# A fused retention and feed-forward kernel: four tiles of the first product by seven products of quarters in two more blocks, and early token sums on GpSimd

## The chip, the cores and the metric

The kernel runs on one core of a Trainium2 chip. The metric is the device time of one execution in microseconds (us); lower is better. A core has five engines that work side by side, each through its own instructions in order: TensorE (PE, matrix products; its weight loads are shown as PEld), VectorE (DVE), ScalarE (ACT), GpSimd (POOL), and SyncE (SP), which here only starts DMA transfers. Matrix products go to PSUM, which has eight banks. A bank can be written anew only when its last reader is done. GpSimd has no part in PSUM here; it works on SBUF alone. Engines wait for each other by semaphores.

## The reference

Two stages. First a retention recurrence over 4 batches, 8 heads, 768 steps and a head width of 64; then a feed-forward layer with a leaky activation over the 3072 tokens:

```python
state = gamma[None, :, None, None] * state + einsum('bhd,bhe->bhde', k[:, :, t], v[:, :, t])
y[:, :, t] = scale * einsum('bhd,bhde->bhe', q[:, :, t], state)
...
x = y.transpose(0, 2, 1, 3).reshape(3072, 512)
h = x @ w_in                                   # 512 -> 2048
g = maximum(h, 0.0) + alpha * minimum(h, 0.0)
out = g @ w_out                                # 2048 -> 512
```

Inputs and output are float32; the kernel computes its products in fp16 and sums them in float32.

## The kernel before

**Tiling.** The retention works in 12 units of 256 steps (three per batch), the feed-forward layer in 6 blocks of 512 tokens, so that a block has two units. While block n goes through its feed-forward products, the two units of block n+1 go through the retention between them. The main loop (line 1188) runs over n from 1 to 5 and writes out by hand in which order every engine gets its instructions.

**First product** (`ffn1`, line 616). Sixteen tiles of 128 features, each four matmuls of 128x512 into one PSUM bank. Behind each tile comes the activation: ACT writes relu(-h) into `hm` (line 648), DVE forms the activated tile in fp16 in `gt` (line 650). The tiles go in the order 0, 8, 1, 9, ... 7, 15, through a list of banks.

**Second product** (`ffn2_seven`, line 826). For blocks 1 to 5 the product of a 512-token block with `w_out` is cut into quarters (two halves of the tokens, features and columns) and done by seven products of quarters in place of eight, after Strassen and Winograd. Each is 16 matmuls of 128x256 (line 857), into the banks named `ox` and `oy`. It needs sums of quarters of the activated tokens, the token sums `gs` (`g_sums`, line 602), numbered 0 to 3; sum 1 needs sum 0, and sum 3 needs sum 1. The third product reads sum 1, the fourth sum 0, the fifth sum 2, the seventh sum 3. In `ffn1` sums 0 and 1 are made by DVE in two halves: over feature tiles 0 to 3 and 8 to 11 behind tile 11, and over the rest behind tile 15. Sum 2 follows in the middle of the second product and sum 3 late in it. Behind the second product ACT copies `ox` to `os` (line 877), which empties the bank for the fourth.

**First product of the last block** (`ffn1_mixed`, line 694). Eight of the 16 tiles are made one by one; the other eight, in two groups of four, by seven products of quarters each, every one of four 128x256 matmuls (line 761). A plan gives the order of tiles and steps: a number is a tile, `a[i]` is step i of a group. Steps 1 and 2 fill one bank, which is then activated as a pair of half tiles; step 1 is also copied by ACT into a second bank, in which steps 6, 7 and 4 add up; ACT copies it out behind 6 and behind 7; step 5 fills a third bank, to which step 3 adds. Two sums with the copies give the other two quarters. The steps need sums of weights (`in_sums`, line 574) and of tokens (`x_sums`, line 590), made by DVE. In the last block the one group's fourth quarter is summed on DVE into SBUF and activated by GpSimd (`prelu_pool`, line 666), and the activated tiles' intermediate results lie in buffers that loads no longer need.

**Retention in the loop.** At the start of an iteration GpSimd rescales k and q of the next two units (line 185, the first one behind `gate`, the block's last token sum) and casts v (`cast_v`, line 201); SP transposes them by DMA (line 205), starts loads, and moves parts of q (line 220). Behind the first of the seven products come the state sums of both units (line 284) and the scores (line 345); from there DVE (`tm`, line 301; `ss`, line 312), GpSimd (`tf`, line 313; copies `tg`, `th`) and ACT (its copies of the same) hand the running state from one to another. The units' results `y` (lines 384 and 398) are copied by ACT into `xT` (line 556), the input of the next block's first product. The next block's first product is begun (`begin`, line 1180) behind the second unit's result, by four matmuls that stand ahead of the sixth of the seven products.

Of the kernel before, what the change touches and what calls it, by code (L numbers as in the profile page):

```python
# [9 lines left out]
FP = mybir.dt.float32  # L10
F16 = mybir.dt.float16
# [11 lines left out]
def kernel(  # L23
# [25 lines left out]
    U = 256  # L49
# [524 lines left out]
    def in_sums(f, i, eng):  # L574

        if f not in win_sums:
            t = sbp.tile([128, H, 2 * D], FP, tag="ks", bufs=3, name=f"wi{f}")
            t = t.rearrange("p h x -> p (h x)").bitcast(F16)
            win_sums[f] = t.rearrange("p (i k c) -> p i k c", i=4, k=2)
        w = w_in_all.rearrange("p (k h) (j f) -> p k h j f", k=2, j=2)[  # L580
            :, :, :, :, 128 * f : 128 * f + 256
        ]
        a11, a21, a12, a22 = (w[:, k, :, j, :] for k in range(2) for j in range(2))
        s1, s2, s3, s4 = (win_sums[f][:, x] for x in range(4))
        o, a, b, op = (
            (s1, a21, a22, ADD), (s2, s1, a11, SUB), (s3, a11, a21, SUB), (s4, a12, s2, SUB)
        )[i]
        return eng.tensor_tensor(out=o, in0=a, in1=b, op=op)

    def x_sums(n, eng):  # L590

        xs = sbp.tile([128, H, 2 * D], FP, tag="ks", bufs=3, name=f"xs{n}")
        xs = xs.rearrange("p h x -> p (h x)").bitcast(F16)
        xs = xs.rearrange("p (i k t) -> p i k t", i=4, k=2)
        x_sum[n] = xs
# [6 lines left out]
    def g_sums(n, i, lo, hi):  # L602
# [10 lines left out]
        last_g.append(nc.vector.tensor_tensor(out=o, in0=a, in1=b, op=op))  # L613
        return last_g[-1]

    def ffn1(n, banks, apart=0):


        turns = [(f, 2, ul, ul + 1) for ul in range(2) for f in range(0, apart, 2)]
        rest = range(apart, NFT)  # L620
        if apart == 0:
            rest = [f + x for f in range(HF) for x in (0, HF)]
        turns += [(f, 1, 0, 2) for f in rest]
        gt = None
        for i, (f0, nf, lo, hi) in enumerate(turns):
            hps = ps(banks[i % len(banks)], "hps").rearrange("p (f t) -> p f t", f=nf)
            parts = [(f, lo, hi) for f in range(nf)]
            if n > 1 and i == 0:
                parts = [(0, 0, 1), (0, 1, 2)]
            for f, ul, uh in parts:  # L630
                for hp in range(4):
                    nc.tensor.matmul(  # L632
                        out=hps[:, f, U * (ul - lo) : U * (uh - lo)].rearrange(
                            "p (u t) -> p u t", t=U
                        ),
                        lhsT=w_in_all[:, hp, 128 * (f0 + f) : 128 * (f0 + f) + 128],
                        rhs=xT[n][:, ul:uh, hp, :],
                        start=(hp == 0),
                        stop=(hp == 3),
                    )  # L640
# [7 lines left out]
            nc.scalar.activation(out=hm, in_=hps, func=RELU, bias=0.0, scale=-1.0)  # L648
# [29 lines left out]
    def prelu(n, f0, lo, hi, hps):  # L678

        nf = hps.shape[1]  # L680
        hm = hms[turn[0] % 4].rearrange("p m e -> p (m e)").rearrange("p (f t) -> p f t", f=nf)
        turn[0] += 1
        nc.scalar.activation(out=hm, in_=hps, func=RELU, bias=0.0, scale=-1.0)
        for f in range(nf):
            nc.vector.scalar_tensor_tensor(
                out=gts[n][:, f0 + f, U * lo : U * hi],
                in0=hm[:, f, :],
                scalar=oma_sb[:, f0 + f : f0 + f + 1],
                in1=hps[:, f, :],
                op0=MULT,  # L690
                op1=ADD,
            )

    def ffn1_mixed(n, plan, banks):
# [12 lines left out]
            return room.pop()  # L707

        def copied(i):
            t = space()  # L710
            nc.scalar.activation(out=t, in_=i, func=COPY, bias=0.0, scale=1.0)
            return t

        hms.extend(space() for _ in range(4))
        for item in plan:
            if isinstance(item, int):
                hps = ps(banks.pop(0), "hps").rearrange("p (f t) -> p f t", f=1)
                for hp in range(4):
# [28 lines left out]
            def x(k, ul):  # L747
# [6 lines left out]
                4: lambda: (bg, w(1, 1), xs[:, 3], False),  # L754
                5: lambda: (bv, wi[:, 0], xs[:, 0], True),
                6: lambda: (bg, wi[:, 1], xs[:, 1], False),
                7: lambda: (bg, wi[:, 2], xs[:, 2], False),
            }[i]()
            for m in range(2):
                for k in range(2):  # L760
# [16 lines left out]
            elif i in (5, 7):  # L777
# [410 lines left out]
    for n in range(1, NBLK):  # L1188
        more = n + 1 < NBLK
        u0 = 2 * (n + 1)  # L1190
        if n > 1:
            gen = begun
            if more:
                for u in (u0, u0 + 1):
# [2 lines left out]
                        behind(i, gate)  # L1197
                    rescale(G, u, 1, 0, 8)
                    turn_dma(u)
                    cast_v(G, u)  # L1200
                    if u > u0:
                        load(u + 1, "qv")
                    else:
                        load(u + 2, "k")
                    move_q(u)
                    tick(gen, 8)
            tick(gen)
            if not more:
                for i in (2, 4):
# [5 lines left out]
        if more and u0 >= MID:  # L1215
# [38 lines left out]
            halves_out(u1, (4, 5), evict=False)  # L1254
            begun = begin(n + 1)
            take_y(u1, (0, 1))
            state_copy(s11, part=1)
            if n == NBLK - 2:
                in_sums(6, 0, V)
                in_sums(6, 1, V)  # L1260
                x_sums(n + 1, V)
                in_sums(4, 0, V)
                in_sums(4, 1, V)
        elif more:
            tick(gen, 16)
            sum_mm(u0, (2, 3))
# [36 lines left out]
        if n == NBLK - 2:  # L1303
            in_sums(6, 2, V)
            in_sums(6, 3, V)
            in_sums(4, 2, V)
            in_sums(4, 3, V)


# [28 lines left out]
```

## Time and profile before

| what | us |
|---|---|
| median of 3 runs | 198.91 |
| lowest and highest of the runs | 198.54 and 199.42 |
| the profiled execution | 198.86 |
| its span, first to last instruction | 196.9 |
| ACT, relu of the first product, 80 of them, mean | 0.597 |
| DVE, token sum over all 8 pairs of tiles (128x2048, fp16) | 1.22 |

The profile is of one execution. Its page gives the busy time of each engine, the chain of work that ended last, and groups of like instructions; from the trace one can ask for a stretch of time, engine by engine. In a group's row stand the source line, the engine, the operation, output and inputs with their shapes, and how often; behind the bar the busy time, the mean duration in nanoseconds, and the idle time of the engine ahead of it with what ended it. In a row of the timeline stand the start and the duration, both in us, and in brackets an idle time ahead of it. In the chain in order of time stand the start, the duration and the work. The granted TensorE clock was 0.997 over the span.

### The profile page before, as it was taken

The page shows a single profiled execution, that of the slowest core. Times are in us where ns is not written, and L with a number is a line of the kernel's source. Part 1 is how long each engine was busy: PE and PEld are TensorE (multiplying, and loading weights), DVE is VectorE, ACT ScalarE, POOL GpSimd, SP SyncE. Part 2 cuts the span into 40 slices and gives each one's busy share as a digit, 9 for nine tenths or more (in the row PEclk, how much of TensorE's full clock was granted, in tenths as well). Part 3 has the DMA queues.
Part 4 walks back from the last instruction along what each step waited for, and adds up shares of the span by engine and source line. Part 5 has one row for each costly group of instructions (what it writes and reads, how often), then busy time and mean ns, then how long its engine had stood idle before and what let it go on. Part 6 is the DMA issues. An engine that isn't in the chain of part 4 may idle for free.

```text
span 196.9 us, 6085 instructions
## 1 busy us (share of the span) xinstructions
PE 189.3 (96%) x2529; PEld 128.8 (65%) x2529; DVE 156.3 (79%) x259; ACT 115.4 (59%) x199; POOL 106.1 (54%) x113
## 2 busy tenths in 40 slices
PE   6688999999999999999999999999999999999993
PEld 2356645568467688744688744788644788865882
DVE  7698987517698998289988389977489996999983
ACT  4458665349187668467467476467466486678110
POOL 3176897499549544970077980076970180039300
PEclk9999999999999999999999999999999999999998
DMA  5999999998879989898988899929865010400014
GB/s 156 313 317 380 374 381 377 293 180 136 211 192 200 286 197 265 213 311 175 213 203 209 256 201 191 222 65 225 256 122 126 17 57 3 160 3 0 0 65 152
DMA packets 90026, 37.92 MB, mean 193 GB/s; under 512 B 57984, under 2 KB 87696, under 8 KB 90000
## 3 DMA queue, kind: packets, MB, share of 16 engines
q1 hardware_dynamic: 88768, 36.45, 69.2%
q0 software_dynamic: 1056, 1.05, 3.6%
q8 instruction: 20, 0.33, 0.6%
q10 hardware_dynamic: 176, 0.04, 0.1%
q14 instruction: 6, 0.05, 0.1%
HBM read 27.31 MB, written 6.29 MB: 171 GB/s over the span
## 4 chain that ended last, share of the span: by engine, by line
PE 90%; SPq 4%; DMA 3%; DVE 0%; issue 0%; POOL 0%; DVEq 0%
PE hps L632 36%; PE ox L857 16%; PE oy L857 12%; PE ops L809 7%; SPq L165 4%; PE hps L719 4%; PE sp L761 3%; DMA vs<-in_v_dram 3%; PE y L533 1%; PE y L384 1%; PE trb L230 1%; PE st L284 1%; PE sca L466 1%; PE ov L857 1%; PE ow L857 1%; PE oz L857 1%
## 5 line engine op out<-in xcount | busy, mean ns | idle before, releaser
L632 PE MATMUL hps<-xT,win 128*128 128x512 f16 (+1 forms) x396 | 71.5, 338 | 0.3 <-DVE ss L423 0.3
L650 DVE SCALAR_TENSOR_TENSOR gt<-hm,oma,hps 128x512 f16<-128x512 f32 (+1 forms) x96 | 59.4, 656 | 12.1 <-issue 4.3
L648 ACT ACTIVATE hm<-hps 128x512 f32<-128x512 f32 x80 | 47.6, 597 | 24.6 <-PE hps L632 22.5
L632 PEld LDWEIGHTS <-win 128*128 128x128 f16 x396 | 38.1, 98 | 31.0 <-POOL win L978 0.4
L857 PEld LDWEIGHTS <-gs 128*128 128x128 f16 x320 | 31.0, 98 | 3.7
L857 PEld LDWEIGHTS <-gt 128*128 128x128 f16 x240 | 22.9, 98 | 4.0
L333 POOL CAST tg<-tm 64x256 f16<-64x256 f32 x12 | 4.8, 396 | 34.3 <-DVE tm L301 22.3
L185 POOL TENSOR_TENSOR kdq<-qs,tab 128x1024 f16<-128x1024 f32 (+1 forms) x12 | 20.2, 1686 | 3.0 <-DVE wsum L572 2.3
L185 POOL TENSOR_TENSOR kdq<-ks,tab 128x1024 f16<-128x1024 f32 (+1 forms) x12 | 20.2, 1686 | 2.6 <-PE y L515 2.6
L857 PE MATMUL ox<-wout,gt 128*128 128x256 f16 x144 | 17.3, 273 | 0.0
L857 PE MATMUL oy<-wsum,gs 128*128 128x256 f16 x144 | 17.2, 273 | 0.0
L556 ACT ACTIVATE xT<-y 128x512 f16<-128x512 f32 x22 | 14.9, 744 | 3.1 <-PE y L533 2.0
L201 POOL CAST vx<-vs 128x1024 f16<-128x1024 f32 (+1 forms) x13 | 12.6, 970 | 6.7 <-DMA vs<-in_v_dram 6.7
L809 PE MATMUL ops<-wout,gt 128*128 128x512 f16 x64 | 15.3, 380 | 0.0
L613 DVE TENSOR_TENSOR gs<-gt 128x1024 f16<-128x1024 f16 (+1 forms) x14 | 13.0, 934 | 0.2
L877 ACT ACTIVATE cu<-oy 128x512 f32<-128x512 f32 x10 | 6.0, 597 | 10.6 <-PE oy L857 10.1
L236 ACT ACTIVATE kq<-trb 128x1024 f16<-128x1024 f16 x8 | 8.2, 1023 | 6.3 <-PE trb L230 6.3
L313 POOL TENSOR_TENSOR tf<-ss,tab 128x256 f32<-128x256 f32 x10 | 10.3, 1028 | 2.5 <-DVE ss L312 1.3
L881 DVE TENSOR_TENSOR os<-ox,cu 128x512 f32<-128x512 f32 x5 | 3.4, 687 | 10.1 <-PE ox L857 10.1
L670 POOL TENSOR_SCALAR hn<-qc,oma 128x256 f32<-128x256 f32 x4 | 4.5, 1138 | 12.4 <-DVE qc L785 12.3
L809 PEld LDWEIGHTS <-gt 128*128 128x128 f16 x64 | 5.8, 98 | 6.0
L424 POOL TENSOR_TENSOR tf<-ss,tab 128x256 f32<-128x256 f32 x6 | 5.9, 980 | 7.1 <-DVE ss L423 7.1
(119 smaller groups left out, 293.1 us busy)
## 6 DMA issues: line engine op xcount, KB each, us to landing
qs<-in_q_dram SPq DMA_DIRECT2D x9, 512.0 KB, 5.4
ks<-in_k_dram SPq DMA_DIRECT2D x32, 128.0 KB, 3.5
vs<-in_v_dram SPq DMA_DIRECT2D x32, 128.0 KB, 4.6
early<-in_moe_w_in_dram SPq DMA_DIRECT2D x7, 512.0 KB, 7.5
out_dram<-os SPq DMA_DIRECT2D x9, 256.0 KB, 2.5
early<-in_moe_w_out_dram SPq DMA_DIRECT2D x4, 512.0 KB, 7.0
out_dram<-ot SPq DMA_DIRECT2D x4, 512.0 KB, 3.8
ks<-in_k_dram SPq DMA_DIRECT2D x6, 256.0 KB, 6.1
```

The costliest lines, as they stand in the source:

```text
L165: nc.sync.dma_start(out=t[nm[0]][:, h, :], in_=src[b, h, U * c : U * c + U, :].rearrange("h (p r) d -> p h (r d)", r=2),)
L185: return eng.tensor_tensor(out=kdq[:, t, :, h0:h1, :].rearrange("p r h d -> p h r d"), in0=staged[u]["kq"[t]][:, h0:h1, :].rearrange("p h ...
L201: eng.tensor_copy(out=o, in_=i)
L236: nc.scalar.activation(out=kq.rearrange("p (x a) i -> p x a i", x=4)[:, :, 2 * hh : 2 * hh + 2, :], in_=trb.rearrange("p (x a i) -> p x a ...
L313: nc.gpsimd.tensor_tensor(out=t, in0=ss, in1=dec, op=MULT)
L556: nc.scalar.activation(out=o, in_=i, func=COPY, bias=0.0, scale=1.0,)
L613: last_g.append(nc.vector.tensor_tensor(out=o, in0=a, in1=b, op=op))
L632: nc.tensor.matmul(out=hps[:, f, U * (ul - lo) : U * (uh - lo)].rearrange("p (u t) -> p u t", t=U), lhsT=w_in_all[:, hp, 128 * (f0 + f) : ...
L648: nc.scalar.activation(out=hm, in_=hps, func=RELU, bias=0.0, scale=-1.0)
L650: nc.vector.scalar_tensor_tensor(out=gt[:, f0 + f, U * lo : U * hi], in0=hm[:, f, :], scalar=oma_sb[:, f0 + f : f0 + f + 1], in1=hps[:, f, :],
L809: nc.tensor.matmul(out=opss[tq], lhsT=gt[:, ft, 128 * tq : 128 * tq + 128], rhs=w_out_all[:, ft, :], start=(ft == 0), stop=(ft == NFT - 1),)
L857: nc.tensor.matmul(out=o[1][m], lhsT=lhs(f, m), rhs=rhs(f), start=(first and f == 0 and (m == 0 or o[0] is None)), stop=(f == HF - 1), ski ...
```

## The change

In blocks 3 and 4 the first product becomes `ffn1_mixed`: twelve tiles one by one, and tiles 4, 5, 12 and 13 by seven products of quarters. The group's way is "d": the fourth quarter is summed by DVE into the bank that steps 1 and 2 have left, and activated as the other quarters are. The sums of weights for this group are made once, by DVE during block 2's first product, into a buffer of their own, and block 5 uses them too; there its own four sums go. The token differences for blocks 3 and 4 are four DVE instructions in buffers of the score masks (`x_sums_apart`), and their last one is now what the rescales wait for. The early half of token sums 0, 1 and 2 is made by GpSimd (`first_sums`), in blocks 2, 3 and 4: behind tile 11. In blocks 3 and 4 that is ahead of tiles 6, 14, 7 and 15; the other half of sums 0 and 1 stays on DVE behind the last tile. The cast of v of the next block's first unit goes from GpSimd to ACT and stands earlier. Step 1 stands ahead of the sixth of the seven products, and tile 0 ahead of the seventh. The banks of the twelve tiles, in the plan's order, are 2, 3, 7, 5, 0, 2, 3, 7, 5, 6, 7, 1; those of the group are 6, 4 and 1.

```diff
@@ in_sums @@
         if f not in win_sums:
-            t = sbp.tile([128, H, 2 * D], FP, tag="ks", bufs=3, name=f"wi{f}")
-            t = t.rearrange("p h x -> p (h x)").bitcast(F16)
-            win_sums[f] = t.rearrange("p (i k c) -> p i k c", i=4, k=2)
+            if f == 4:
+                win_sums[f] = sbp.tile([128, 4, 2, U], F16, tag="wi4", name="wi4")
+            else:
...
+    def x_sums_apart(n):
+
+        b = xT[n].rearrange("p j (k a) t -> p j k a t", k=2)
+        t = [
+            sbp.tile([128, 512], F16, tag=f"m2{i % 2}{i // 2}", bufs=2, name=f"xs{i}")
+            for i in range(4)
+        ]
+        xs = x_sum[n] = [x.rearrange("p (k t) -> p k t", k=2) for x in t]
+        for o, x, y in (
+            (xs[0], b[:, 1, 0], b[:, 0, 0]),
+            (xs[1], b[:, 1, 1], xs[0]),
+            (xs[2], b[:, 1, 1], b[:, 1, 0]),
+            (xs[3], b[:, 0, 1], xs[1]),
+        ):
+            i = nc.vector.tensor_tensor(out=o, in0=x, in1=y, op=SUB)
+        return i
+
+    def first_sums(n):
+
+        for i in range(3):
+            g_sums(n, i, 0, 4, nc.gpsimd)
@@ ffn1 @@
-                lo = 0 if apart or f0 < NFT - 1 else 4
-                hi = HF if f0 == NFT - 1 else 4
-                g_sums(n, 0, lo, hi)
-                g_sums(n, 1, lo, hi)
+                if apart:
+                    g_sums(n, 0, 0, HF)
+                    g_sums(n, 1, 0, HF)
+                elif f0 < NFT - 1:
+                    first_sums(n)
+                else:
+                    g_sums(n, 0, 4, HF)
+                    g_sums(n, 1, 4, HF)
@@ ffn1_mixed @@
         for item in plan:
+            if item == "first":
+                first_sums(n)
+                continue
...
-                if (f, 5) in sums and (f, 7) in sums:
+                if (f, 5) in sums and (f, 7) in sums and "d" in item[3]:
+                    h22 = ps(at[0], "h22").rearrange("p (f t) -> p f t", f=2)
+                    nc.vector.tensor_tensor(
+                        out=h22, in0=sums.pop((f, 5)), in1=sums.pop((f, 7)), op=ADD
+                    )
+                    done.append((f + HF, 1, 2, h22))
...
         for t in done:
             prelu(n, *t)
+        if n < NBLK - 1:
+            g_sums(n, 0, 4, HF)
+            g_sums(n, 1, 4, HF)
@@ the plan and begin @@
+    a = steps(4, 6, 4, 1, "d")
+    PLAN = [a[1], 0, a[2], 8, a[6], 1, a[5], 9, a[7], 2, 10, a[3], 3, a[4], 11, "first", 6, 14, 7, 15]
+    BANKS = (2, 3, 7, 5, 0, 2, 3, 7, 5, 6, 7, 1)
+    MIXED = (3, 4)
...
+        if n in MIXED:
+            gen = ffn1_mixed(n, PLAN, BANKS)
+            tick(gen, 3)
+            return gen
@@ the main loop @@
-                    cast_v(G, u)
+                    if u > u0 or n not in MIXED:
+                        cast_v(G, u)
...
+            if n == 2:
+                tick(gen, 4)
+                for i in range(4):
+                    last_g.append(in_sums(4, i, V))
...
-            g_sums(n, 2, 0, HF)
+            g_sums(n, 2, 4, HF)
...
             take_y(u1, (0, 1))
+            if n + 1 in MIXED:
+                tick(begun, 1)
...
-                in_sums(4, 0, V)
-                in_sums(4, 1, V)
+            if n + 1 in MIXED:
+                cast_v(A, u0 + 2)
+                gate = x_sums_apart(n + 1)
+                tick(gen, 16)
+                tick(begun, 4)
```

More of the change, by code (lines that the diff above doesn't have):

```diff
@@ L576, in in_sums @@
         if f not in win_sums:
-            t = sbp.tile([128, H, 2 * D], FP, tag="ks", bufs=3, name=f"wi{f}")
-            t = t.rearrange("p h x -> p (h x)").bitcast(F16)
-            win_sums[f] = t.rearrange("p (i k c) -> p i k c", i=4, k=2)
+            if f == 4:
+                win_sums[f] = sbp.tile([128, 4, 2, U], F16, tag="wi4", name="wi4")
+            else:
+                t = sbp.tile([128, H, 2 * D], FP, tag="ks", bufs=3, name=f"wi{f}")
+                t = t.rearrange("p h x -> p (h x)").bitcast(F16)
+                win_sums[f] = t.rearrange("p (i k c) -> p i k c", i=4, k=2)
         w = w_in_all.rearrange("p (k h) (j f) -> p k h j f", k=2, j=2)[
@@ L594, in x_sums @@
         xs = xs.rearrange("p (i k t) -> p i k t", i=4, k=2)
-        x_sum[n] = xs
+        x_sum[n] = [xs[:, i] for i in range(4)]
         b = xT[n].rearrange("p j (k a) t -> p j k a t", k=2)
@@ L600, in x_sums, with g_sums @@
         eng.tensor_tensor(out=xs[:, 3], in0=b[:, 0, 1], in1=xs[:, 1], op=SUB)
-    def g_sums(n, i, lo, hi):
+    def x_sums_apart(n):
[13 more added lines that the diff above has]
+        return i
+    def g_sums(n, i, lo, hi, eng=None):
         if n not in gsums:
@@ L612, in g_sums @@
         )[i]
-        last_g.append(nc.vector.tensor_tensor(out=o, in0=a, in1=b, op=op))
+        last_g.append((eng or nc.vector).tensor_tensor(out=o, in0=a, in1=b, op=op))
         return last_g[-1]
+    def first_sums(n):
+        for i in range(3):
+            g_sums(n, i, 0, 4, nc.gpsimd)
     def ffn1(n, banks, apart=0):
@@ L680, in prelu @@
         nf = hps.shape[1]
-        hm = hms[turn[0] % 4].rearrange("p m e -> p (m e)").rearrange("p (f t) -> p f t", f=nf)
-        turn[0] += 1
+        if n == NBLK - 1:
+            hm = hms[turn[0] % 4].rearrange("p m e -> p (m e)")
+            turn[0] += 1
+        else:
+            hm = sbp.tile([128, TB], FP, tag="hm", bufs=3, name="hm")
+        hm = hm.rearrange("p (f t) -> p f t", f=nf)
         nc.scalar.activation(out=hm, in_=hps, func=RELU, bias=0.0, scale=-1.0)
@@ L709, in copied @@
         def copied(i):
-            t = space()
+            if n == NBLK - 1:
+                t = space()
+            else:
+                t = sbp.tile([128, 2, HM], FP, tag="cu", bufs=OUTS["cu"], name="cu")
             nc.scalar.activation(out=t, in_=i, func=COPY, bias=0.0, scale=1.0)
             return t
-        hms.extend(space() for _ in range(4))
+        if n == NBLK - 1:
+            hms.extend(space() for _ in range(4))
         for item in plan:
+            if item == "first":
+                first_sums(n)
+                continue
             if isinstance(item, int):
@@ L753, in ffn1_mixed @@
                 3: lambda: (bv, wi[:, 3], x(1, 1), False),
[L754 to L757, printed above, removed]
+                4: lambda: (bg, w(1, 1), xs[3], False),
+                5: lambda: (bv, wi[:, 0], xs[0], True),
+                6: lambda: (bg, wi[:, 1], xs[1], False),
+                7: lambda: (bg, wi[:, 2], xs[2], False),
             }[i]()
@@ L782, in ffn1_mixed @@
                     sums[f, 5] = copied(bv) if p else bv
-                if (f, 5) in sums and (f, 7) in sums:
+                if (f, 5) in sums and (f, 7) in sums and "d" in item[3]:
[4 more added lines that the diff above has]
+                    done.append((f + HF, 1, 2, h22))
+                elif (f, 5) in sums and (f, 7) in sums:
                     h22 = space()
```

2 lines of the change are left out of this document (removed).

## The prediction

> **What bounds the kernel now.** I read the page's busy shares and its chain of work first, then the chain in order of time around block 3, then the queues of VectorE (DVE), GpSimd (POOL) and ScalarE (ACT) there.
>
> ```profile
> PE 189.3 (96%) x2529; PEld 128.8 (65%) x2529; DVE 156.3 (79%) x259; ACT 115.4 (59%) x199; POOL 106.1 (54%) x113
> PE 90%; SPq 4%; DMA 3%; DVE 0%; issue 0%; POOL 0%; DVEq 0%
> ```
> ```profile
> 107.06 0.54 PE hps L632 x4
> 107.60 1.75 PE oy L857 x16
> 109.34 1.75 PE ox L857 x16
> 111.09 13.39 PE hps L632 x64
> 124.48 1.78 PE ox L857 x16
> ...
> 127.16 1.85 PE ox L857 x16
> 129.02 1.75 PE oy L857 x16
> 130.76 0.87 PE ox L857 x8
> ...
> 135.32 0.27 PE y L384 x17
> ```
>
> TensorE is the chain: from block 2 on its matmuls follow each other without a gap worth naming. So work taken from it counts only if nothing else then comes late, and the other queues must be tested for slack. In these rows 107.60 is the sixth product of block 2, 109.34 its seventh, 111.09 the first product of block 3, 124.48 the first of block 3's seven products, and 130.76 the first half of its fourth.
>
> ```profile
> 125.93 0.69 DVE L613 TENSOR_TENSOR gs<-gt 128x1024 f16<-128x1024 f16 x1
> 126.65 0.69 DVE L613 TENSOR_TENSOR gs<-gs,gt 128x1024 f16<-128x1024 f16 x1
> 127.26 0.41 DVE L301 TENSOR_TENSOR tm<-tf,st 128x256 f32<-128x256 f32 x1
> ...
> 128.92 0.42 DVE L301 TENSOR_TENSOR tm<-tf,st 128x256 f32<-128x256 f32 x1 [0.19 <-POOL tf L313]
> ```
> ```profile
> 127.74 0.39 POOL L333 CAST tg<-tm 64x256 f16<-64x256 f32 x1 [10.47 <-DVE tm L301]
> 128.28 0.61 POOL L313 TENSOR_TENSOR tf<-ss,tab 128x256 f32<-128x256 f32 x1
> ```
> ```profile
> 129.38 0.41 ACT L329 ACTIVATE tg<-tm 64x256 f16<-64x256 f32 x1
> 129.82 0.60 ACT L877 ACTIVATE os<-ox 128x512 f32<-128x512 f32 x1
> ```
>
> This is the tight place. Behind the first product the queues hand one thing round: the two token sums of the second half (DVE, 125.93 and 126.65), tm (DVE, 127.26), tf (POOL, 128.28), tm again (DVE, 128.92), its copy tg (ACT, 129.38), and only then, in ACT's queue, the copy os that empties the bank of ox. It ends at 129.82 + 0.60 = 130.42, and the fourth product needs that bank at 130.76: slack 0.34. POOL was idle for 10.47 us before that chain; the change fills that idle time.
>
> **The change part by part.** *TensorE, removed.* In each of blocks 3 and 4, four tiles of four 128x512 matmuls become seven products of four 128x256 matmuls: 16 go, 28 come. From the rows, 256 columns cost 1.75/16 = 0.109 and 512 cost (13.39 - 4 x 0.109)/60 = 0.216. So 16 x 0.216 - 28 x 0.109 = 0.39 us less per block, 0.8 for two. That is all there is to win: 198.86 - 0.8 = 198.1.
>
> *DVE, added in the first product.* Durations come from block 5, where the same steps run already:
>
> ```profile
> 177.92 0.69 DVE L790 TENSOR_TENSOR sp<-sp,qc 128x512 f32<-128x512 f32 x1
> 178.53 0.86 DVE L685 SCALAR_TENSOR_TENSOR gt<-qc,oma,sp 128x256 f16<-128x256 f32 x2
> 179.31 0.74 DVE L685 SCALAR_TENSOR_TENSOR gt<-qc,oma,hps 128x512 f16<-128x512 f32 x1
> 179.97 0.86 DVE L685 SCALAR_TENSOR_TENSOR gt<-qc,oma,sp 128x256 f16<-128x256 f32 x2
> ```
>
> Start to start: a sum in PSUM 0.61, a pair of halves 0.78, a whole tile 0.66. Four tiles at 0.66 give way to four pairs at 0.78 and two sums at 0.61, +1.7; the two early token sums (0.69 each) leave, -1.4. The total hardly moves, but the order does. The steps a2, a6, a5 give DVE little while TensorE runs them, and the adds and pairs come together behind a7. Step by step: TensorE ends the sixth product at 109.34, tile 0 (0.86) at 110.2, the seventh product at 111.96; a2, 8, a6, 1, a5, 9 (three of 0.44, three of 0.86) end at 115.86; a7, 2, 10, a3, 3, a4, 11, 6, 14 (three of 0.44, six of 0.86) end at 122.34.
>
> ```profile
> L648 ACT ACTIVATE hm<-hps 128x512 f32<-128x512 f32 x80 | 47.6, 597 | 24.6 <-PE hps L632 22.5
> L236 ACT ACTIVATE kq<-trb 128x1024 f16<-128x1024 f16 x8 | 8.2, 1023 | 6.3 <-PE trb L230 6.3
> 107.13 1.34 ACT L556 ACTIVATE xT<-y 128x512 f16<-128x512 f32 x2
> ```
>
> DVE gets tile 9 one relu (0.60) later, at 116.5, and has no gap from there: 9, sum, 2, pair, 10, sum, 3, pair, pair, 11 = 4 x 0.66 + 2 x 0.61 + 3 x 0.78 + 0.74 = 6.94, with some 0.2 for hand-overs, so tile 11 is done at 123.65. **Tile 7 takes tile 11's bank (7)**, and TensorE is there at 122.34: it waits 1.5, to about 123.85 with the hand-over. Tiles 7 and 15 end at 125.6, where before it was 124.48.
>
> *POOL, added: three token sums over half the tiles.* They start behind tile 11, at 123.7.
>
> ```profile
> L572 POOL TENSOR_TENSOR wsum<-wout 128x2048 f16<-128x2048 f16 x1 | 4.1, 4064 | 0.0
> 107.83 1.90 POOL L185 TENSOR_TENSOR kdq<-ks,tab 128x1024 f16<-128x1024 f32 x1
> 130.65 1.22 DVE L613 TENSOR_TENSOR gs<-gt 128x2048 f16<-128x2048 f16 x1
> 130.91 1.44 POOL L313 TENSOR_TENSOR tf<-ss,tab 128x256 f32<-128x256 f32 x1 [0.17 <-POOL tg L333]
> ```
>
> The nearest row, fp16 pairs, gives 4.06/2 = 2.03 each; the other sum of 1024 took 1.90. I take 2.03 and keep 1.90 and, from tf's 0.61 for 256, 2.45 as ends. The last two rows show more: tf, 0.61 alone, took 1.44 when it met an fp16 sum on DVE and ended 0.47 behind that sum, so the two kinds of sum exclude each other. Here the POOL sums run 123.7 to 125.75 and to 127.8. DVE's sum over the second half, due at 127.0 behind tile 15, waits to 127.8 and runs to 128.5; the third POOL sum follows to 130.5; DVE's other one starts there. Before, it started at 126.65 and os ended 3.77 later; now os ends at 134.27, and the fourth product, with the old hand-over of 0.2, starts at 134.4 in place of 130.76: **+3.65 per block**. The bank wait and a wait of the third product lie inside that. Behind it nothing of DVE or POOL is nearer than before, so it is not won back. Blocks 3 and 4 have the same rows: 7.3.
>
> The Trainium skill speaks against this edit (SBUF — State Buffer, section "SBUF: two separate sides"): a DVE instruction with two SBUF inputs and a GpSimd one hold their shared ports for the whole instruction, and the other blocks. By it the sum is the one above; without it the POOL sums would end at 129.8, DVE's would lie beside them, and tg, tf, tm, tg and os would follow to 132.4: 1.8 per block. The Trainium skill (GPSIMD Engine Reference, section "3.1 Elementwise — side-by-side cycle accounting") has 4497 ns for an fp32 sum of 2048; by half of that, 2.25, the estimate would be some 1.3 us higher.
>
> *Block 2.* Its early sums go to POOL and four sums of weights come to DVE, three tiles earlier.
>
> ```profile
> L588 DVE TENSOR_TENSOR wi<-win 128x512 f16<-128x512 f16 x4 | 1.7, 416 | 0.0
> ```
>
> Four of 0.42 against two of 0.69 is +0.3, in front of the reuse of a bank; 0.2 taken, 0 and 0.6 kept. POOL's three sums fit there: it is done with its casts well before the eighth tile. In block 5 those weight sums leave DVE:
>
> ```profile
> 168.84:181.42 12.58, 12.58 (x86) 8.21 (x85) 12.51 (x28) 10.06 (x19) 5.92 (x6) 1.00 0.16 58
> ```
>
> The columns are the stretch, then TensorE, weight loads and DVE busy: TensorE is gapless at 12.58 of 12.58, so this wins nothing.
>
> *Moved.* The cast of v goes to ACT (about 1.02 by the 1024 row) between the copies of xT, over at 108.47, and tile 0's relu: with a copy of 0.60, a small one and the old copy of 0.60, ACT is free near 111.0, and DVE reaches tile 0 by 111.6, ahead of the seventh product's end. Nothing waits. The rescales on POOL stay behind the gate, now the last token difference, four DVE instructions of 0.42 behind xT: 110.2 in place of 107.83, so they end near 118.8, still 5 us ahead of the sums.
>
> ```profile
> 112.33 2.30 SPq L205 DMA_TRANSPOSE kq<-kdq x1
> ...
> 124.18 1.29 SPq L220 DMA_DIRECT2D qf<-kq x2
> ```
>
> Their consumers in SP's queue (transposes, then loads, then the moves of q) slide by about 2 us, the last q to 127.5 plus its landing; it is read at 135.32 or later. Hidden; if not, each us over costs one.
>
> Sum: 198.86 + 7.3 + 0.2 = 206.4, rounded down to **206.2** for the shorter POOL row. The profiled execution took 198.86, its span 196.9, and the median of the runs is 198.91, so nothing is to be shifted.
>
> **The rivals.** (a) *Only the bank wait.* The POOL sums and DVE's do not exclude each other, or POOL is faster on contiguous fp16. Then per block the bank's 1.5 less 0.39 stays, up to 1.8 with the late tf: 198.86 + 2.2 to 3.6 + 0.2 = 201.3 to 202.7. For it: no row shows two such sums of 1024 meeting. Against it: the 1.44. (b) *Nothing waits*, the other side: the late order of DVE is caught up, as in block 5, where DVE is busy 12.51 of 12.58 and TensorE has no gap. It decides at bank 7: DVE must end tile 11 by about 122.2, 1.4 us sooner than I count, and the POOL sums must be done by 127.7. Then 198.1, the whole saving. Against it: 6.94 us of instructions stand between, and the wait for tile 7's activation is already met today, the 1.78 at 124.48 where other products take 1.75. (c) *POOL slower* (2.45 each): 1.3 more per block, 208.9.
>
> **How the numbers follow.** The forecast has 0.52, (a) with what lies between it and the forecast 0.25, (b) 0.16, (c) 0.03; 0.04 is left for a gain from a source that I do not see. A difference under 0.5%, about 1.0 us, can't be told from none here, so (b) counts as the same. Faster 0.04, same 0.16, slower 0.80. The range takes in (a) and the bounds of the POOL sum short of (c): 200.8 to 208.2.
>
> **What would show it.** Right: tile 7's first matmul waits over 1 us for tile 11's activation; each POOL token sum takes about 2.0; a DVE token sum behind them waits or is stretched; the fourth product starts late behind os. Wrong: first product of 12.9 us without gap, or POOL sums near 1 us, or tm within 2 us of the last tile's activation.

## The result and the profile after

The changed kernel takes **207.83 us** (median, 207.42 to 208.05) against 199.16 (198.54 to 199.45) for the kernel before in the same comparison: a ratio of **1.044, interval 1.040 to 1.047**. It is slower, where the forecast was 206.2 with a range of 200.8 to 208.2. The profiled execution took 208.05, its span is 206.0, and the granted clock was 1.0.

First the page of the changed kernel: busy time by engine, then the shares of the chain that ended last.

```profile
PE 190.8 (93%) x2545; PEld 130.5 (63%) x2545; DVE 163.4 (79%) x273; ACT 119.1 (58%) x207; POOL 122.5 (60%) x120
...
PE 72%; DVE 13%; issue 4%; ACT 4%; DMA 3%; SPq 2%; POOL 1%; ACTq 0%; POOLq 0%
```

TensorE had 90% of the chain before; now DVE and ACT stand in it. Where they stand in it is shown by the view of what TensorE waited for between 78 and 180 us, that is in blocks 2 to 4 (in total, times, longest). For the kernel before, this view is empty in that stretch.

```profile
PE ox L906 <- ACT os L926: 3.2, 2, 1.6
PE hps L759 <- DVE gt L718: 3.0, 2, 1.6
PE oy L906 <- DVE gs L633: 1.3, 2, 0.7
PE hps L657 <- DVE gt L675: 0.6, 1, 0.6
```

The three waits that come twice are one per block in blocks 3 and 4: the fourth product for `os`, tile 7 for the activation in its bank, the third product for a token sum. The last row, 0.6 once, is in block 2. The chain of the changed kernel in order of time:

```profile
78.22 0.54 PE hps L657 x4
...
108.09 0.54 PE sp L801 x4
...
122.77 2.32 DVE gt L718 x5
...
125.13 1.90 PE hps L759 x8
127.06 0.61 ACT hm L716
127.69 0.76 DVE gt L718
128.47 1.58 DVE gs L633
130.11 2.38 issue
132.49 0.42 DVE tm L301
...
135.03 0.61 ACT os L926
...
135.68 1.03 PE ox L906 x8
...
141.02 0.54 PE sp L801 x4
...
173.67 0.54 PE sp L801 x4
...
202.53 0.02 issue
```

The rows of 0.54 are the four matmuls with which a block begins; from one to the next is the **length of a block**. This is the measure for all that follows, since the stages ahead of block 2 end somewhat differently in every execution (its beginning lies between 77.1 and 78.8 in the runs below). Before, the blocks 2, 3, 4 and 5 began at 78.10, 107.06, 135.94 and 164.80, and the last product ended at 193.66. So block 2 took 28.96 and takes 29.87 (+0.91), block 3 28.88 and 32.93 (+4.05), block 4 28.86 and 32.65 (+3.79), and block 5 28.86 both times, 202.53 - 173.67 now. With 0.12 ahead of block 2 that is the 8.87 by which the last product ends later.

How a block loses it is seen in the queues around the end of block 3's first product, DVE's first, then GpSimd's (start, duration, work, idle time ahead).

```profile
124.34 2.06 DVE L718 SCALAR_TENSOR_TENSOR gt<-hm,oma,hps 128x512 f16<-128x512 f32 x3
...
128.47 1.57 DVE L633 TENSOR_TENSOR gs<-gt 128x1024 f16<-128x1024 f16 x1
130.07 2.49 DVE L633 TENSOR_TENSOR gs<-gs,gt 128x1024 f16<-128x1024 f16 x1
132.49 0.41 DVE L301 TENSOR_TENSOR tm<-tf,st 128x256 f32<-128x256 f32 x1
```
```profile
111.17 1.90 POOL L185 TENSOR_TENSOR kdq<-ks,tab 128x1024 f16<-128x1024 f32 x1 [2.36 <-DVE xs L619]
...
118.60 1.04 POOL L201 CAST vx<-vs 128x1024 f16<-128x1024 f32 x1
125.16 2.12 POOL L633 TENSOR_TENSOR gs<-gt 128x1024 f16<-128x1024 f16 x1 [5.53 <-DVE gt L718]
127.36 2.12 POOL L633 TENSOR_TENSOR gs<-gs,gt 128x1024 f16<-128x1024 f16 x1
129.45 2.56 POOL L633 TENSOR_TENSOR gs<-gt 128x1024 f16<-128x1024 f16 x1
```

Tile 11's activation is the first of the three at 124.34 and ends at 125.08; GpSimd has waited 5.53 for it and begins at 125.16. From there its three sums follow each other. DVE wants its own sum at 128.47, but that takes 1.57 in place of 0.69 and ends at 130.04, when GpSimd's second sum has ended; GpSimd's third then takes 2.56 in place of 2.12, and DVE's second 2.49. The two engines take turns, and `tm`, which stood at 127.26 before, comes at 132.49. Then `os` ends at 135.63 and the fourth product begins at 135.68.

### The profile page after: what moved, and what is told of

Its sections match the earlier page's. It is cut to its first block, busy times and chain, and to the rows that moved or that the text cites. A ratio compares the mean times of both kernels' runs of the same rounds, so it can differ in the third digit from the quotient of the medians.

```text
span 206.0 us, 6145 instructions
## 1 busy us (share of the span) xinstructions
PE 190.8 (93%) x2545; PEld 130.5 (63%) x2545; DVE 163.4 (79%) x273; ACT 119.1 (58%) x207; POOL 122.5 (60%) x120
## 4 chain that ended last, share of the span: by engine, by line
PE 72%; DVE 13%; issue 4%; ACT 4%; DMA 3%; SPq 2%; POOL 1%; ACTq 0%; POOLq 0%
PE hps L657 18%; PE ox L906 12%; PE oy L906 10%; PE hps L759 9%; PE ops L858 7%; DVE gt L718 5%; PE sp L801 5%; DMA ks<-in_k_dram 3%; ACT hm L716 2%; DVE gs L633 2%; SPq L165 2%; PE y L533 1%; DVE gt L675 1%; PE trb L230 1%; DVE wi L591 1%
## 5 line engine op out<-in xcount | busy, mean ns | idle before, releaser
L657 PE MATMUL hps<-xT,win 128*128 128x256 f16 (+1 forms) x260 | 43.3, 324 | 0.7 <-DVE gt L675 0.6
L675 DVE SCALAR_TENSOR_TENSOR gt<-hm,oma,hps 128x256 f16<-128x256 f32 (+1 forms) x64 | 36.3, 611 | 9.6 <-issue 4.3
L673 ACT ACTIVATE hm<-hps 128x512 f32<-128x512 f32 x48 | 28.4, 596 | 14.0 <-PE hps L657 11.3
L657 PEld LDWEIGHTS <-win 128*128 128x128 f16 x260 | 25.0, 98 | 17.4 <-issue 1.2
L759 PE MATMUL hps<-xT,win 128*128 128x512 f16 x128 | 30.7, 379 | 3.0 <-DVE gt L718 3.0
L906 PEld LDWEIGHTS <-gt 128*128 128x128 f16 x240 | 22.9, 98 | 4.0
L718 DVE SCALAR_TENSOR_TENSOR gt<-hm,oma,hps 128x512 f16<-128x512 f32 x24 | 17.5, 744 | 6.3 <-ACT hm L716 6.0
L633 POOL TENSOR_TENSOR gs<-gt 128x1024 f16<-128x1024 f16 x6 | 13.6, 2272 | 14.3 <-DVE gt L718 10.8
L759 PEld LDWEIGHTS <-win 128*128 128x128 f16 x128 | 12.5, 98 | 14.8 <-issue 3.5
L716 ACT ACTIVATE hm<-hps 128x512 f32<-128x512 f32 x24 | 14.3, 597 | 6.8 <-PE hps L759 5.4
L201 POOL CAST vx<-vs 128x1024 f16<-128x1024 f32 (+1 forms) x11 | 10.5, 960 | 6.3 <-DMA vs<-in_v_dram 6.2
L633 DVE TENSOR_TENSOR gs<-gt 128x1024 f16<-128x1024 f16 (+1 forms) x11 | 11.4, 1047 | 0.1
```

The source lines that it names most:

```text
L201: eng.tensor_copy(out=o, in_=i)
L633: last_g.append((eng or nc.vector).tensor_tensor(out=o, in0=a, in1=b, op=op))
L657: nc.tensor.matmul(out=hps[:, f, U * (ul - lo) : U * (uh - lo)].rearrange("p (u t) -> p u t", t=U), lhsT=w_in_all[:, hp, 128 * (f0 + f) : ...
L675: nc.vector.scalar_tensor_tensor(out=gt[:, f0 + f, U * lo : U * hi], in0=hm[:, f, :], scalar=oma_sb[:, f0 + f : f0 + f + 1], in1=hps[:, f, :],
L718: nc.vector.scalar_tensor_tensor(out=gts[n][:, f0 + f, U * lo : U * hi], in0=hm[:, f, :], scalar=oma_sb[:, f0 + f : f0 + f + 1], in1=hps[: ...
L759: nc.tensor.matmul(out=hps[:, 0, :].rearrange("p (u t) -> p u t", t=U), lhsT=w_in_all[:, hp, 128 * item : 128 * item + 128], rhs=xT[n][:, ...
```

## The experiments

**Theory**, from the prediction's steps: the early sums on GpSimd exclude DVE's sums of the second half and delay `os` by their turns; DVE's order makes the activations late; the bank of tile 7 costs nothing by itself, because the chain to `os` ends behind it anyway. **Rivals:** the bank wait is the cost; or GpSimd's sums cost by themselves, wherever they stand; or the cost is in work that one more block of quarters brings in any order. In the diffs "-" is the changed kernel unless something else is said. The median of the kernel before beside these runs was 198.5 to 198.7.

| run | median us | ratio to before (interval) | block 2 | block 3 | block 4 |
|---|---|---|---|---|---|
| before (profile ahead of the prediction) | 199.16 | 1 | 28.96 | 28.88 | 28.86 |
| changed kernel | 207.83 | 1.044 (1.040 to 1.047) | 29.87 | 32.93 | 32.65 |
| e1_bank | 207.14 | 1.045 (1.039 to 1.050) | 30.88 | 32.92 | 32.65 |
| e2_dve | 204.79 | 1.031 (1.027 to 1.034) | 30.63 | 31.43 | 31.01 |
| e4_insum | 209.92 | 1.057 (1.053 to 1.062) | 28.9 | 36.2 | 32.66 |
| e6_pool_sums_only | 198.62 | 1.000 (0.997 to 1.003) | 29.03 | 28.87 | 28.83 |
| e7_insum_ahead | 206.49 | 1.039 (1.035 to 1.043) | 29.03 | 32.93 | 32.65 |
| e8_order_pool | 200.60 | 1.010 (1.007 to 1.013) | 29.17 | 29.79 | 29.79 |
| e9_order_dve | 200.03 | 1.007 (1.004 to 1.010) | 28.96 | 29.62 | 29.62 |
| e10_one_block | 203.33 | 1.024 (1.020 to 1.028) | 29.57 | 32.93 | 28.83 |
| e11_os_first | 198.69 | 1.001 (0.999 to 1.003) | 29.09 | 28.84 | 29.08 |
| e12_os_order | 198.20 | 0.998 (0.997 to 1.000) | 28.96 | 28.64 | 29.08 |

The lengths are of the one profiled execution of each run, from its chain in order of time; that execution need not be the median one.

**1. Is it the bank?** Tile 7 goes to bank 2, which is long free.

```diff
-    BANKS = (2, 3, 7, 5, 0, 2, 3, 7, 5, 6, 7, 1)
+    BANKS = (2, 3, 7, 5, 0, 2, 3, 7, 5, 6, 2, 1)
```

> The changed kernel with one number altered: tile 7 goes to bank 2 (empty since tile 10) in place of bank 7. Theory (the late chain: tile 11's activation, three GpSimd sums, DVE's sums of the second half, tm, tf, tm, tg, os, fourth product): the wait of tile 7 (about 1.5 us per block) goes, but the first, third and fourth products wait as much longer, so 207.8 within 0.7. Rival (the bank is the cost): both waits are won, about 3 us, 204.7.

Measured 207.14 (206.95 to 209.18). What TensorE waited for in the same stretch:

```profile
PE ox L906 <- ACT os L926: 3.2, 2, 1.6
PE oy L906 <- DVE gs L633: 2.3, 2, 1.2
PE ox L906 <- DVE gt L718: 1.9, 2, 1.0
```

The 3.0 for the bank are gone, and blocks 3 and 4 are as long as before the edit to a hundredth: 32.92 and 32.65. TensorE gets 1.5 further on average, and then waits as much longer: 1.0 per block for the last activation, ahead of the first of the seven products, and 0.5 more for the third product's sum. The largest wait that could be removed by one number was worth nothing. (Block 2, which the edit doesn't touch, had a wait of 1.6 in this execution, the slowest of the run's four; see 4.)

**2. Is it GpSimd's sums?** They go back to DVE, at the same place in its order; sum 2 is made whole, as before the change.

```diff
-        for i in range(3):
-            g_sums(n, i, 0, 4, nc.gpsimd)
+        for i in range(2):
+            g_sums(n, i, 0, 4)
...
-            g_sums(n, 2, 4, HF)
+            g_sums(n, 2, 0, HF)
```

> The changed kernel with the early half of token sums 0 and 1 back on DVE, in their new place behind tile 11, and sum 2 whole on DVE in its old place, in blocks 2 to 4. Theory (GpSimd's late sums set the fourth product): the waits behind os and for the token sums go, the bank wait stays and DVE's two sums of 0.69 push tile 7's activation, so about 3.3 us are won: 204.5 (203.5 to 205.5). Rival (the seven products' order on DVE is all of the cost, GpSimd none): no gain or a loss, 207.8 or more.

Measured 204.79. DVE's queue at the end of block 3's first product in this run:

```profile
124.76 0.69 DVE L633 TENSOR_TENSOR gs<-gt 128x1024 f16<-128x1024 f16 x1
125.48 0.69 DVE L633 TENSOR_TENSOR gs<-gs,gt 128x1024 f16<-128x1024 f16 x1
...
128.84 0.69 DVE L633 TENSOR_TENSOR gs<-gt 128x1024 f16<-128x1024 f16 x1
129.57 0.69 DVE L633 TENSOR_TENSOR gs<-gs,gt 128x1024 f16<-128x1024 f16 x1
```

All four sums take 0.69 again, and the wait for `os` is gone: 1.50 and 1.64 us less in the two blocks, although DVE does more. (Block 2, where DVE now has both these sums and the sums of weights, took 0.76 more than in the changed kernel.) But 2.6 and 2.2 over the kernel before remain, and in the view of waits they are now tile 7's for its bank (1.5 per block on average) and one of 0.8 per block in which the first of the seven products waits for a last activation. So there are two chains that are late beside each other, GpSimd's and DVE's own, and the later one sets the end; their lateness doesn't add up.

**3. Do GpSimd's sums cost by themselves?** Here "-" is the kernel before: its plain tiles stay, and only the early sums 0, 1 and 2 of blocks 2 to 4 go to GpSimd.

```diff
-                g_sums(n, 0, lo, hi)
-                g_sums(n, 1, lo, hi)
+                if apart == 0 and f0 < NFT - 1:
+                    for x in range(3):
+                        g_sums(n, x, 0, 4, nc.gpsimd)
+                else:
+                    g_sums(n, 0, lo, hi)
+                    g_sums(n, 1, lo, hi)
...
-            g_sums(n, 2, 0, HF)
+            g_sums(n, 2, 4, HF)
```

> The kernel before with one part of the change alone: the early half of token sums 0, 1 and 2 on GpSimd in blocks 2, 3 and 4, with the plain 16 tiles. There tile 11 is the eighth tile, so GpSimd starts some 5 us earlier, against the end of the first product. Theory (the sums cost because they start late): the sums end before DVE's of the second half are due, DVE is relieved, 198.6 to 199.2, no loss. Rival (sums on GpSimd cost by themselves, by their 2.1 us each and by shutting DVE out): 201 or more.

Measured 198.62, ratio 1.000 (0.997 to 1.003), and no wait of TensorE in blocks 2 to 4. GpSimd's queue in block 3, and DVE's first sum of the second half:

```profile
118.67 2.13 POOL L613 TENSOR_TENSOR gs<-gt 128x1024 f16<-128x1024 f16 x1 [1.78 <-DVE gt L650]
120.87 2.13 POOL L613 TENSOR_TENSOR gs<-gs,gt 128x1024 f16<-128x1024 f16 x1
122.95 2.13 POOL L613 TENSOR_TENSOR gs<-gt 128x1024 f16<-128x1024 f16 x1
```
```profile
125.53 0.69 DVE L613 TENSOR_TENSOR gs<-gt 128x1024 f16<-128x1024 f16 x1
```

They begin 12.0 behind the block's beginning (118.67 - 106.66) and end at 125.08, ahead of DVE's sums at 125.53. In the changed kernel they begin 17.07 behind it. The same instructions cost nothing there, while here 1.5 to 1.6 per block are won when DVE makes them: it is the place, not the engine. Run e8 (6) tests this in the changed kernel itself.

**4. Block 2.** Its wait of 0.6 was put down to the four sums of weights, which are ahead of the reuse of a bank. First they were moved to the end of block 2, behind the token differences.

```diff
-            if n == 2:
-                tick(gen, 4)
-                for i in range(4):
-                    last_g.append(in_sums(4, i, V))
...
                 gate = x_sums_apart(n + 1)
+                if n == 2:
+                    for i in range(4):
+                        in_sums(4, i, V)
                 tick(gen, 16)
```

> The changed kernel with the four sums of weights taken from block 2's first product and put behind the token differences for block 3, where DVE is idle. Theory: TensorE's wait in block 2 (0.6 us for a bank, 0.9 by the block's end) goes and blocks 3 and 4 stay, 207.0 (206.8 to 207.3). Rival (block 2's delay comes from its GpSimd sums): no change, 207.8.

Measured 209.92: **a miss**, by 3 us, and slower than the changed kernel. Block 2 did lose its wait, but block 3 grew by 3.2, with two new waits of TensorE of 1.5 each for DVE. DVE's queue, then GpSimd's, at its beginning:

```profile
109.83 0.41 DVE L591 TENSOR_TENSOR wi<-win 128x512 f16<-128x512 f16 x1
110.28 2.01 DVE L591 TENSOR_TENSOR wi<-wi,win 128x512 f16<-128x512 f16 x1
112.21 2.12 DVE L591 TENSOR_TENSOR wi<-win 128x512 f16<-128x512 f16 x1
114.26 2.12 DVE L591 TENSOR_TENSOR wi<-win,wi 128x512 f16<-128x512 f16 x1
```
```profile
109.99 2.02 POOL L185 TENSOR_TENSOR kdq<-ks,tab 128x1024 f16<-128x1024 f32 x1 [2.25 <-DVE xs L619]
111.97 2.08 POOL L185 TENSOR_TENSOR kdq<-qs,tab 128x1024 f16<-128x1024 f32 x1
```

The token differences are the gate of the rescales. So the edit let the rescales go (1.90 each) and put 0.42-us sums right beside them: three of the four sums waited for a whole rescale. That was not foreseen, and it is the clearest view of the exclusion in this case. The next run puts the same sums ahead of the gate in place of behind it.

```diff
-            if n == 2:
-                tick(gen, 4)
-                for i in range(4):
-                    last_g.append(in_sums(4, i, V))
...
             if n + 1 in MIXED:
+                if n == 2:
+                    for i in range(4):
+                        in_sums(4, i, V)
                 cast_v(A, u0 + 2)
                 gate = x_sums_apart(n + 1)
```

> The changed kernel with the four sums of weights moved to the end of block 2, now ahead of the token differences, which the GpSimd rescales wait for; so no rescale can run beside them. Theory (a DVE sum with two SBUF inputs waits for a whole GpSimd instruction): each takes about 0.4, block 2's wait of TensorE goes, blocks 3 and 4 stay: 206.9 (206.6 to 207.3). Rival (the place at the end of block 2 is bad in itself, as in the run where they stood behind the differences): 209 or more.

Measured 206.49, a little under its range: block 2 back at 29.03, blocks 3 and 4 unchanged at 32.93 and 32.65. The sums cost block 2 what they did because of whom they met there. In the changed kernel, DVE and GpSimd:

```profile
87.48 1.28 DVE L591 TENSOR_TENSOR wi<-win 128x512 f16<-128x512 f16 x1
```
```profile
87.45 1.04 POOL L201 CAST vx<-vs 128x1024 f16<-128x1024 f32 x1
```

The first sum was shut out by the cast of v, 1.28 in place of 0.42. The cost differs between executions with the place of GpSimd's work: in e10 the first sum took 0.98, and in e1 two sums were stretched, to 1.57 and 1.14. TensorE's wait for the bank follows this stretch: 0.3 for 0.56 (e10), 0.6 for 0.86 (here), 1.6 for 1.87 (e1). Block 2 took 29.57 to 30.88 in the four profiled executions that have the sums there, 28.90 to 29.17 in all others.

**5. One block alone.** `MIXED = (3,)`, so block 4 is plain.

> The changed kernel with the seven products in block 3 alone; block 4 has its 16 plain tiles and keeps GpSimd's early sums. Theory (each block pays by itself, about 3.8 to 4.0 us): 203.8 (203.3 to 204.3). Rival (block 4 pays because block 3 left it late, or the other way): outside of that by over 1 us.

Measured 203.33. Block 3 is 32.93 as in the changed kernel, block 4 28.83 as before it. The cost belongs to the block that has the quarters, and the block behind neither wins nor loses by it.

**6. Is it the order?** Both of these have the sums of weights as in e7, and another plan: the group's steps and tiles in another order, so that DVE's adds and pairs don't come together at the end. Banks are chosen to fit. In both, the diff shows the plan alone. In e8 the sums stay on GpSimd, with tiles 0 to 3 and 8 to 11 early, so that it can begin earlier:

```diff
-    PLAN = [a[1], 0, a[2], 8, a[6], 1, a[5], 9, a[7], 2, 10, a[3], 3, a[4], 11, "first", 6, 14, 7, 15]
+    PLAN = [a[1], 0, a[6], a[2], 1, 3, 8, 2, 10, 11, 9, a[5], a[7], "first", 6, 7, 14, a[3], a[4], 15]
```

In e9 all early sums are DVE's, as in e2, and stand at the end, with the steps early:

```diff
-    PLAN = [a[1], 0, a[2], 8, a[6], 1, a[5], 9, a[7], 2, 10, a[3], 3, a[4], 11, "first", 6, 14, 7, 15]
+    PLAN = [a[1], 0, a[6], a[2], a[5], a[7], 9, 6, 8, 1, a[3], a[4], 11, 3, 2, 7, 15, 10, 14, "first"]
```

> As the run with the weight sums ahead of the differences, and the plan in another order with other banks: tiles 0 to 3 and 8 to 11 come first, GpSimd's sums behind them, so that they start some 3.5 us earlier; the steps 3 and 4 come late. All instructions are the same. Theory (what costs is when the GpSimd sums start and which bank waits, not how much is done): no GpSimd sum meets a DVE sum, no bank wait, what is left is DVE's backlog in front of tm, about 0.9 to 1.5 per block: 200.8 (200.0 to 202.0). Rival (seven products in these blocks cost by themselves, whatever the order): 204.5 or more.

> As the run before, but with the early sums 0 and 1 on DVE and a plan in which the steps come first and plain tiles last. Theory (DVE's work up to tm is the floor: GpSimd's help with the early sums is worth little once the order is right): 200.5 (199.8 to 202.0), within 1 us of the order with GpSimd. Rival (GpSimd's sums are the cost in any order): 198.5, faster than the other order by over 1.5 us. Rival (GpSimd's relief is needed): 203 or more.

Measured 200.60 and 200.03; blocks 3 and 4 went from 32.9 and 32.7 to 29.79 and 29.62. In e8, GpSimd's queue and DVE's in block 3:

```profile
121.31 2.12 POOL L633 TENSOR_TENSOR gs<-gt 128x1024 f16<-128x1024 f16 x1 [1.17 <-DVE gt L718]
123.51 2.13 POOL L633 TENSOR_TENSOR gs<-gs,gt 128x1024 f16<-128x1024 f16 x1
125.59 2.14 POOL L633 TENSOR_TENSOR gs<-gt 128x1024 f16<-128x1024 f16 x1
```
```profile
127.92 0.69 DVE L633 TENSOR_TENSOR gs<-gt 128x1024 f16<-128x1024 f16 x1
128.64 0.69 DVE L633 TENSOR_TENSOR gs<-gs,gt 128x1024 f16<-128x1024 f16 x1
```

GpSimd's last sum ends at 127.73, ahead of DVE's first: no collision, 2.12 to 2.14 and 0.69 throughout. So **most of the loss was the order of the plan** with its banks, 3.1 of 4.05 in block 3, and it holds with the sums on either engine. What is left in e9 is the fourth product's wait for `os`, 0.6 per block, and one of 0.2 for a last activation, ahead of the first of the seven products. (The expectation for e11 calls the second one the third product's.)

**7. Can it be had for nothing?** In ACT's queue `os` stands behind one copy `th` and the second `tg`, which it doesn't need. In e11 it is put ahead of them, in addition to e9; e12 has another plan on top, so that DVE is done with the pairs some seven tiles before the end (eight in block 3 of its trace). In the second diff "-" is e11's plan, which is that of e9; the banks are again chosen to fit.

```diff
             tick(gen, 8)
             middle_copy(m00, 1)
+            tick(gen, 8)
             state_copy(s00, part=1)
             middle_copy(m01, 1)
-            tick(gen, 9)
+            tick(gen, 1)
```
```diff
-    PLAN = [a[1], 0, a[6], a[2], a[5], a[7], 9, 6, 8, 1, a[3], a[4], 11, 3, 2, 7, 15, 10, 14, "first"]
+    PLAN = [a[1], 0, a[6], a[2], a[5], a[7], 11, 2, a[3], a[4], 7, 9, 3, 1, 10, 6, 8, 14, 15, "first"]
```

> The order of e9, with one more step: in ACT's queue of the second product the copy os stands directly behind the first tg, ahead of the copies th and the second tg. Theory: in e9 (200.03) the only waits of TensorE in blocks 3 and 4 that are left and do not stand in the kernel before are the fourth product's for os, 0.6 per block, and the third product's for DVE's sum, 0.2 per block. os has no need of th and tg, 0.4 to 0.6 each, which stand ahead of it. So os's wait goes: 200.03 - 1.2 = 198.8, from 198.3 to 199.3, which is the kernel before (198.7) within what can be told: the saving of 0.8 on TensorE pays for block 2's slower stretch and no more. Rival 1, the copies that are now behind os delay the retention's state, and its scores wait for them in place of os: no better than e9, 199.7 to 200.3. Rival 2, with nothing waiting the change shows its whole saving of 0.8: 197.6 to 198.1.

> As e11, with another order of the twelve tiles and the steps: tiles 11 and 2 between the group's steps 7 and 3, and the tiles without a sum to wait for at the end, so that DVE is done with the group's pairs seven tiles before the end of the first product. Theory: the first product has no wait in e9 already, so the order only changes when DVE starts its token sums; the 0.2 per block of the third product goes too: 198.4, from 198.0 to 199.0. Rival 1, as in e11 the delayed copies cost what os gains: 199.5 or more. Rival 2, the new order makes a new wait for a bank in the first product: 199.5 or more, with a wait of hps on gt in the rows of blocks 3 and 4.

Measured 198.69 and 198.20, ratios of 1.001 (0.999 to 1.003) and 0.998 (0.997 to 1.000): the 8.7 us are won back, with the quarters kept and the early sums back on DVE. The 0.2 for the last activation, still there in e11, is gone in e12. Against the kernel before, e12 comes out 0.2% lower, which can't be told from no change by this measurement: its interval reaches to 1.000. All that TensorE still waits for in blocks 2 to 4 of e12 is this one row, in block 4:

```profile
PE oy L906 <- ACT xT L556: 0.4, 1, 0.4
```

And the windows of e12 (stretch, its length, then busy time of TensorE, weight loads, DVE, ACT and GpSimd; at the end the granted clock, the DMA engines' share and GB/s) over blocks 3 and 4 and within the two first products show how little room is left:

```profile
107.00:180.00 73.00, 72.58 (x977) 51.72 (x975) 64.92 (x121) 52.06 (x95) 34.00 (x36) 1.00 0.55 135
113.00:123.50 10.50, 10.50 (x56) 5.17 (x54) 10.38 (x19) 8.25 (x14) 5.68 (x4) 1.00 0.98 193
142.00:152.50 10.50, 10.50 (x56) 5.32 (x55) 10.40 (x20) 8.35 (x15) 4.62 (x3) 1.00 0.60 137
```

In the first products DVE is busy 10.38 and 10.40 of 10.50, and TensorE all of it. The saving is there where nothing waits: block 3 took 28.64 in place of 28.88. Block 4 took 29.08, 0.22 over; there the chain runs through DVE from the first tiles to the state and its copies, and ends in `xT`.

## Why the prediction was right

Step by step, with the numbers counted from the beginning of block 3 (107.06 before, 108.09 after).

- **TensorE's saving, 0.39 per block:** the first product without a wait (e12) takes 13.59, which is 0.54 for step 1, 0.86 for tile 0 and 12.19 for the rest, against 13.39 + 0.54 = 13.93: **0.34**. Over the whole block 0.24 of it arrived in e12's block 3. The step holds, as an upper bound.
- **DVE's order and the bank:** tile 11's activation was forecast to end at 16.59 and ended at 16.99; tile 7's wait 1.5, measured 1.6 and 1.4 in the two blocks. That it lies inside the wait for `os`, as the prediction had it, is shown by e1.
- **GpSimd's sums and the exclusion:** forecast in turns, POOL, POOL, DVE, POOL, DVE, and that is the order of the rows. The size of one was put at 2.03 and measured **2.12**, and 2.20 from the first start to the second. GpSimd also began 0.43 later than forecast (17.07 for 16.64). The fourth product came 27.59 behind the block's beginning in place of the forecast 27.34; before it was 23.70. So +3.89 for +3.65, and **+4.05 and +3.79** over the whole blocks. (The forecast's hand-over of 0.2 from `os` to the product is in no row before, where TensorE came 0.34 behind `os`; measured, it is 0.05.) The Trainium skill (SBUF — State Buffer, section "SBUF: two separate sides") has the whole instruction shut out, not slowed: the trace agrees, the sum of 0.69 ended 0.56 behind the end of GpSimd's second sum at 129.48, and in e4 each of three sums of 0.42 took as long as the rescale beside it. The prediction's estimate from the Trainium skill (GPSIMD Engine Reference, section "3.1 Elementwise — side-by-side cycle accounting"), 2.25 per sum, was too high by 0.13.
- **Not won back, and nothing in block 5:** right; no wait of TensorE stands behind the fourth product's in blocks 3 and 4, block 5 is 28.86 before and after, and e10's block 4 is a plain block's length.
- **Moved work costs nothing:** right. The rescales begin 3.08 behind the block's beginning, forecast 3.14, and GpSimd then stands idle for 5.53; no wait for a transpose or for q is in the view of waits.
- **Block 2, +0.2 (0 to 0.6):** this term was **mis-sized**. It was 0.91, of which 0.75 in the first product (14.14, from 82.26 to 96.40, in place of 13.39). The sums of weights were priced at 0.42 each, and the exclusion, which the prediction applied to block 3, was not applied to them: the cast of v beside them made the first 0.86 longer, and the bank's reuse felt it.

So the sum of 7.5 was short by 1.4 of the 8.87 measured: 0.71 from block 2, 0.54 from the two blocks (4.05 + 3.79 - 7.3), and 0.12 from what lies ahead of block 2, of which nothing was forecast.

Rival (a), only the bank wait, is out: the sums of the two engines do exclude each other (1.57 and 2.49 in place of 0.69), and with another bank (e1) nothing changes. Rival (c) had the right direction and too large a price. Rival (b), that nothing waits, is false for this plan, and e11 and e12 show under which conditions it nearly becomes true: pairs early, all early token sums on DVE, the sums of weights ahead of the gate, `os` ahead of the copies. Even then the saving of 0.8 doesn't come: block 3 gives 0.24, and block 4 takes 0.22 back.

What stays open: whether block 4's last 0.4 can be removed by yet another order; no run tried it. In e8's blocks 0.9 remain, where TensorE waits 0.7 for ACT's copy `oy` behind the late last pair, and up to 0.2 for `os`; how much of that comes of the late pair and how much of the sums on GpSimd was not separated.

## What to carry to other kernels

When a saving on the bounding engine is paid for with work on other engines, one of which is busy for 79% of the span, count first when the last instruction of each queue in that stage ends, not how much it adds: here 0.3 to 0.4 us of saving per block were paid with 4 us of lateness, and the order alone gave 3 of them back. A large wait in the list need not be worth anything (1.5 per block for tile 7's bank, nothing gained without it) where two late chains lie beside each other; compare the lengths of whole blocks. Before a two-input sum is moved on DVE, look at what GpSimd has at that time, and at what the moved instruction itself releases.

## What the runs showed of the hardware

- An fp16 sum of two SBUF operands on DVE waits for a whole GpSimd instruction, and the profile shows that wait as duration: 0.42 became 2.01 to 2.12 beside rescales of 2.02 and 2.08 (e4), and 1.28 beside a cast of 1.04 (changed kernel). So the cast, which has one operand, shuts it out as well.
- GpSimd is shut out as well: its third sum took 2.56 with a DVE sum ahead of it (changed kernel), and 2.13 and 2.14 without (e6, e8).
- DVE's activations, which read one operand from PSUM, don't meet this: in e8 they took 0.74 and 0.75 for a tile while GpSimd was in its sums.
- A GpSimd sum of two fp16 operands with 1024 columns takes 2.12 to 2.14 when nothing shuts it out (changed kernel, e6, e8), and the next begins 2.1 to 2.2 after it began. DVE takes 0.69 for the same size, about a third.
